# Attention's and memory's parts added by GpSimd instead of VectorE, with a newly searched instruction order

## The chip, the cores and the metric

The kernel runs on one core of a Trainium2 chip. The metric is the device time in microseconds (us) of one execution. Five engines work side by side, each through its own queue in order: TensorE (PE in the profile; PEld is its weight loads), VectorE (DVE), ScalarE (ACT), GpSimd (POOL) and SyncE (SP, which here only starts DMAs). SBUF is the on-chip memory, PSUM the memory that matmuls write. bf16 is a 16-bit float.

## The reference

Two independent parts share one output of 2048 x 1280. Part A (the first 640 columns) is a short convolution of `k`, a product with `v`, a convolution over the whole sequence done with FFTs, and a product with `q`. Part B (the last 640) is attention in four segments of 512 tokens, 32 heads of 20, with a memory that carries over from the earlier segments:

```python
for s in range(N):                       # N = 4 segments, L = 512
    logits = einsum('bhqd,bhkd->bhqk', qs, ks) * scale + mask
    p = softmax(logits)
    a_dot = einsum('bhqk,bhkd->bhqd', p, vs)
    pq = phi(qs)                         # phi(t) = t + 1 if t > 0 else exp(t)
    num = einsum('bhld,bhde->bhle', pq, M)
    den = einsum('bhld,bhd->bhl', pq, z) + 1e-06
    a_mem = num / den
    o = g * a_mem + (1.0 - g) * a_dot    # g = sigmoid(beta), one per head
    ...
    M = M + einsum('bhld,bhle->bhde', phi(ks), vs)
    z = z + sum(phi(ks))
return o @ wo
```

In segment 0 the memory is empty, so the sum `o` has one part only. In segments 1 to 3 it has two: these are the sums of the title.

## The kernel before, in words

A recording layer first collects all instructions, with what each depends on. Then two tables of numbers, `ORDER` and `BASE`, found by a search over a planner's costs, set the order in which they are issued on all engines and the PSUM banks they use. Every instruction is issued by one helper, so the profile shows line 256 for nearly all; tiles tell them apart. A third table, `EVICT`, says for each of the 227 copies from PSUM to SBUF whether DVE ("1") or ACT ("0") makes it.

Part A runs in five blocks of 128 columns (`conv`). `kr`, `kb` and `skd` are the short convolution, `vt` its product with v; `F` holds the spectrum as it leaves PSUM, `Xh` and `Kh` the two spectra after butterflies, `Y` and `pq` their product, and a last pass multiplies by q into `pq`, which a DMA writes out. All the butterflies and products are DVE work, mostly on two SBUF tensors of 1024 to 4096 elements in each partition.

Part B runs in eight units (`u`: segment `s`, half of the heads). `project` makes k and q (`KQ`) and v (`Va`) by matmul, copies them out of PSUM, and turns k and q around by DMA (`KQT`); `PP` and `PqT` are phi of k and q, `qabs`, `kam` and `A` a bound for the softmax. `attend` fills PSUM with logits, ACT takes their exponential into `ET` (128x1024 at a time, 160 of them), and PE multiplies by `Va` and by the memory `Mbd`. For each group of four heads `normalise` closes: a reciprocal of the denominators (`rr`), one product from PSUM into `o2` (the profile calls this tile `o`; it holds both parts, 2 x 320 elements, there is one buffer of it), and the sum of the two halves into `o_s`. `project_out` turns `o_s` around (by DMA in segments 0 to 2, by PE with the identity in the last, into `xT`), multiplies by `wo` and copies the result into `outb`, in the last segment also into `PP`, for the DMA out.

The sum stands once in each of the six units of segments 1 to 3 for each of the four groups of heads, so 24 times. POOL has only start-up work before the change: four DMAs (`outb` first receives beta, `qabs` the short filter) and the memsets.

Of the kernel before, what the change touches and what calls it, by code (L numbers as in the profile page):

```python
# [264 lines left out]
class Layer:  # L265
# [482 lines left out]
    def attend(self, u):  # L748
        nc, rec = self.nc, self.rec
        V = nc.vector  # L750
        s, half = u // 2, u % 2
# [114 lines left out]
        def normalise(gg, g, nb, step):  # L866
            rec.key = ("N", u, gg)
            h0 = 16 * half + 4 * gg
            pov = g.ap[:, 0:nb, 0:352].rearrange("p b (x e) -> p b x e", e=VW)
            rr = self.ring("rr", [128, 66], f32)[:, 0:16 * nb].rearrange("p (b x) -> p b x", x=16)  # L870
            den = pov[:, :, :, 0]
            part, bank, cell = [list(x) for x in den.ap] if nb > 1 else (None, None, None)
            if nb > 1:
                den = bass.AP(tensor=den.tensor, offset=den.offset, ap=[part, [512 + step, nb], cell])
            V.reciprocal(out=rr, in_=den, grp=g)
            num = pov[:, :, :, 1:DH + 1]
            if s == 0:
                dst = o_s[:, :, h0:h0 + 4 * nb, :].rearrange("p q (b h) e -> p b q h e", b=nb)
                V.tensor_tensor(out=dst, in0=num.rearrange("p b (q h) e -> p b q h e", h=4), in1=rr.rearrange("p b (q h) -> p b q h", h=4)[:, :, :, :, None].to_broadcast([128, nb, 4, 4, DH]), op=ALU.mult, grp=g)
            else:  # L880
                o2 = self.ring("o2", [128, 2, 16, DH])
# [28 lines left out]
    def project_out(self, s):  # L910
# [79 lines left out]
ORDER = r"""  # L990
c-jTQ17H{c3<SVW@|kUSwr$&9XWO=I+qOCz?QGk&&ATkf3P(0%M-JpfB;*2+A7v2{xlszyP#Mut0p(B)QBfLIkOyf{0A)}JF%S!R5gFwXfH=s2il~Yx2!(toh~!!cDO3<2hCE8dL`}p-UhRT(S{Oy32t
+Mp)lA5yDK&#uM-6mCDy@S=NR8S^fb5zU^^jg0pc(3-FEXPm3Tu57(dGz^Bxr>;D5~*L0vWYCiXn%#Kr*yOBNWpn$fs?QTYI7*ifcc#L<#MU#^`~P+7wwd9onH6@@s1CgZAivuo#H6nnpXKKZ>H14n=Z
wMkmBYLKM;hIvAz3j1IzR3`0&Gf{{ptFc^Tb7=z&$g|a$LGwBo^hY=W$;uxm0wV;;MZJ4f^bvr8PaNU9OI#yGnfo8;JghMW!fT=nWlduz$F-OPg6g1S5n2xzxRV!*Eor+32Pj_Lwj?fvXrqy+VPQyqIL
JfVam9>`cM->g!QCd@HVmA(;jyBfC+C)cdZQYAmSg6gluI|AiZL0gQM4Raht*7;M4rb~>oJ0#fgxOfC9rP5E;w&cX7@e<M(NSBf+5&B*=P(zMq?4L0)6)pSJoME0I0M=d{L<dqS{Gos_ENXwXrn81A!c
be{jJfghc3cOU5fCw1t+iq6Lpn#*Q02w%P>i!$T4iv)w&!}EV{MVc6t~~5Y-~sAKk2Lw2uzZff`wY(OK7Oc=Xl3dL3PLF}i42izYX5AN_QY4%YMNua|HE>-8cw>Sb)u+X!b@Fhn2XD&kpeTc=TFHEv+2
-oj%%!Wuk599xMnwnv}h0m4aiiEOJ7L*m+c+`(RbhW#2-_UT>3w}W~Q8<4=(B9<kx1G-J0ql2wOfQjwUv)a*KAdbY6xUv!3^(D^fCM32XJ+E6ep2U_U_6l3HpLMdG+TS``YYQ*CHNLz-1RT*_n$%t+x&
2dEB1tUC?2xvxcQ~r2G%=3pTLj2yO<`yBum)=q3DM))My}}zeUFrOQa_-lwX_IwU2o`Rjc73}m0iOpw6fH4MI+fqT-D@qK|dp=rI3{J6)hw^5?Vy*ZeP&LE^2DKq@gU0+|;}J4QcF_-qZUU+HPwqNo$#
{xAm|e$ZARDjy}+T_>PB~#gfS{q?JCFK+;JzODK;tyZyya46t;T#|GMOw3Qr2NpE?ri)FBGme2mcCA|!>u9nd<*-#s1Z7qYev;5XkAbDkwWs(9`&_o7XU&|+jETiO>!lrV`ikL}G3nh7ExMh|Rmdmn8Q
E4YRrLYu~+?HQPS}_YPqbvoATQMmjB`lYWu?|wwidrEVYc;Kal(Ovd-2$z>WtGx4)5cjXt7h$Gmc6tbGTuJe536Cq>h{ViTXC6SVdSGJe_9u*VkKmv^^mGoN+#K4`(<UVla!RM(oK5G6dP@wrJPl;^7h
)EXm=?sQ>~1Il{fa!Dp?<yX8ok1^%Zcom6N&FU&`1gt8I1cv(>dZHr-}eDAu#r+EVJ<GY!oKw$K{cb8T#8rJ=piCf3vzSu=Z~i_O`PVc6W}SvZE}5Sec+?5%#Ym-^lo*gO4eN2NWNTX?o$BYv^+(t#1V  # L1000
!iGvq4v>|$#8z20S#1?$jXl+Y^3@`-lB~7gw#=5Aah<i2KUPs9GXl38d0Yb7jK^fXRhIhPU^{Jx?X~8tDh(Kgy(B94+ddm6(K$jkS~b~Zn{A|=kRXf3+T3DQq_=FfT{c{*%O3lxHRP=gk{EoiyX~DFww
SCf!PZ(rtS!H5U1`T7_Ct@_E3GBRY_J@+nml0Nv=$FqO^L;LJY;d$ij8@~x^s%mkU*&;+iaAaw9|IR&RQFuv(YkE;_`!bVQY?&_-w+d(vjn2lGI^rcI9}PCm(gDbmC-5!1LCWb$QAb$b9L>3)VyuahjZ
!gq$v?Bq@7vp`4eK(o~Z3qW#p)?8)9dCv&8pB;zcZE3>5!FGv6zNn$491Ubz5l7fpQCHt}-8%RGkmc!Ce`tvPQ@f}lhAk*;$(=a`k%1aJlT4vx9SuBH?k$L!@gLzRhF)#CRnLJ}=HkajcNt#I^e&BsRX
JJ0%1LkKDKH>@~z#GiUUR)_dn2p()gSS|amn~R|G7EF^CWrI1tdiR-&RiVEGctn3Sb{_Og{4`BWjT_$xmwEczFd{^tiV#dD{JH_OY)OGkZV$rW4Tt!_(b{2&w5YpSS40w6;|aqe&%?N;t_enb@GkXc*X
8oS-)kkIEJJ7gZFq@Ub8xH%LbXi8m#5F?TTENpPa;*EbQy$i%w*q&tehZD6<(Nb2ynd<c@5Yn=+MiS=4`V9&gDsPT?k*!H@jSivEe4Wjc3AG5^Eswu+VfhCP(kEahvsO&-Zs`Od$b&jnn_MO@6%{*PN^
E#X13j_X;&mvAY?E4%x0uHa5t$;WbsHT|uqKamZ5CQs!qzsoMUXH|S7H*vSTlV=vzpUYKyA@pV3BhT%nY~>HRX5rm@ue_4_{#wHMHtv(ntmkheh}*e?A7u+0_)fl;lKw$<v626j&+<t^`B(WR`=zmekp
uFWVf>r?mI%I^q5YvX@ja~TH|+`kNJM{Rk$f-raX%w_RDWVo`~VN~sa5x;p3?uxAvW{WUcvuLIgjS4yoKMlU`F?t{=#B;Y>(rj&=~%}%6l?T?#=y>#Pt;3(yMwrZ{-IijVJJgp2$txc!0<Ew4T^cQ}wZ
>^J<>n&+sIVFo|dMOrF6{F@#5%#oKvS&*s@Zhf~k8hiCSr-r9S)>oMl^T;A4u`enBF;|#5N`~<Hsly>yIp3fV4ZqM%>yptFAa}1*eyt8-l^9-k5J*-|}3Ge0wy|#zfI^Nr(X?MTKe%{~v_$3bTfj-Im`
c+2IK|a|F`CuR8Q+&0L^N2dshxu?H;n%pv$9q&A;$uCEuJkxM!K3R)ALXljhDX-KI?-qQb;i|MKF8<!XrJeiG>K02`99MZ_*!4*F*K%5^JE%NW9f8X=!-moF7_q9)R*~kkFD!{g>UdZ9$%B{5l^UleWP
#oM7qfXG|2b)Q9tGfeT(n+t$xUl`(Z!e+kJ<h@L=EOJ3YjA`ELIYeKp$N  # L1010
"""
# [76 lines left out]
```

## Time and profile before

| | |
|---|---|
| time, median of 3 runs | 271.66 us (271.04 to 272.06) |
| profiled execution, span | 271.3 us; no other time is given for it |
| PE, DVE, ACT, POOL busy | 96%, 91%, 92%, 3% |
| granted TensorE clock | 1.000 |
| DVE: `o` products | 24, 820 ns mean |
| DVE: `o_s` sums of `o` | 24, 316 ns mean |
| ACT: `ET` exponentials | 160, 1113 ns mean |

The profile's busy time is the time in which an engine has at least one instruction under way. Instructions of one engine overlap a little: the next starts before the one ahead has ended. What an instruction costs its engine in a full stretch is therefore read from start to start, and is less than its duration. A row of the timeline gives the start (us), the time (us; several merged ones together), the engine, the line, the operation, out<-in, shapes and a count.

### The profile page before, as it was taken

What the parts mean: (1) busy time and instruction counts of PE and PEld (TensorE: products, weight loads), DVE (VectorE), ACT (ScalarE), POOL (GpSimd) and SP (SyncE); (2) the same over time, 40 slices, a digit from 0 to 9 for tenths busy, and PEclk for the clock granted to TensorE, in tenths of its full rate; (3) what the DMA queues carried; (4) which work ended last, traced back from release to release, by engine and by line L of the source; (5) the groups of instructions that cost most, each with busy time, mean ns of one, the idle gap of its engine ahead of it and who ended that gap; (6) DMA issues with size and microseconds to landing.
All of it is one profiled execution on the core that took longest, in us unless ns stands there. A gap on an engine that the chain in (4) does not pass through costs nothing.

```text
span 271.3 us, 10053 instructions
## 1 busy us (share of the span) xinstructions
PE 259.8 (96%) x4335; PEld 194.0 (71%) x4335; DVE 246.4 (91%) x385; ACT 249.7 (92%) x394; POOL 7.2 (3%) x18
## 2 busy tenths in 40 slices
PE   6999999999999999999999999999999999988994
PEld 2688768877767677877767788778776776565772
DVE  0268999999999999999999999999999999999972
ACT  2676899999899999999999999999999999999952
POOL 8200000000000000000000000000000000000000
PEclk9999999999999999999999999999999999999999
DMA  6997989999999869997997679996970094635124
GB/s 196 274 217 143 235 178 208 190 243 258 211 164 262 189 153 169 156 183 153 172 219 156 180 148 216 162 170 123 201 165 17 30 159 99 154 89 126 47 51 126
DMA packets 131516, 44.72 MB, mean 165 GB/s; under 512 B 121899, under 2 KB 129072, under 8 KB 131344
## 3 DMA queue, kind: packets, MB, share of 16 engines
q1 hardware_dynamic: 131328, 43.96, 80.0%
q8 instruction: 34, 0.56, 0.9%
q0 software_dynamic: 144, 0.12, 0.2%
q14 instruction: 10, 0.08, 0.1%
HBM read 14.05 MB, written 7.34 MB: 79 GB/s over the span
## 4 chain that ended last, share of the span: by engine, by line
PE 66%; ACT 18%; DMA 8%; SPq 3%; issue 2%; DVE 2%; ACTq 0%; DVEq 0%
PE ps L256 66%; ACT ET L256 12%; DMA Wi<-c_wi 3%; SPq L256 3%; ACT F L256 2%; DMA Y<-in_B_x_dram 2%; DMA KQT<-qabs 1%; ACT Va L256 1%; DMA pq<-in_A_q_dram 1%; ACT outb L256 1%; ACT KQ L256 1%; DVE PP L256 1%; ACT PP L256 1%; DVE o L256 0%; DVE outb L256 0%
## 5 line engine op out<-in xcount | busy, mean ns | idle before, releaser
L256 ACT ACTIVATE ET<-ps 128x1024 bf16<-128x1024 f32 x160 | 162.4, 1113 | 0.4 <-PE ps L256 0.4
L256 PE MATMUL ps<-wqkv,xT 128*128 128x320 bf16 x480 | 78.2, 302 | 0.6 <-ACT ET L256 0.3
L256 PEld LDWEIGHTS <-xT 128*128 128x128 bf16 x640 | 58.0, 98 | 28.8 <-issue 7.1
L256 ACT CAST F<-ps 128x512 bf16<-128x512 f32 x72 | 43.9, 683 | 1.3 <-PE ps L256 1.3
L256 PE MATMUL ps<-Va,ET 128*128 128x21 bf16 x1280 | 41.9, 173 | 0.0
L256 PEld LDWEIGHTS <-ET 128*128 128x128 bf16 x1280 | 39.3, 96 | 3.3 <-issue 2.1
L256 PE MATMUL ps<-KQT 32*128 32x128 bf16 (+2 forms) x896 | 34.8, 239 | 0.6 <-DMA KQT<-qabs 0.4
L256 PEld LDWEIGHTS <-Wf 128*128 128x128 bf16 x320 | 29.6, 98 | 6.5 <-issue 1.6
L256 ACT CAST KQ<-ps 128x320 bf16<-128x320 f32 x56 | 26.7, 522 | 1.8 <-PE ps L256 1.8
L256 PE MATMUL ps<-wo,xT 128*128 128x320 bf16 (+2 forms) x160 | 25.5, 299 | 1.3 <-ACT ET L256 1.3
L256 PEld LDWEIGHTS <-KQT 32*128 32x128 bf16 x896 | 16.5, 92 | 10.1 <-issue 7.6
L256 PE MATMUL ps<-kT,Wf 128*128 128x256 bf16 x160 | 22.2, 273 | 0.0
L256 PE MATMUL ps<-vt,Wf 128*128 128x256 bf16 x160 | 21.6, 273 | 0.2
L256 PE MATMUL ps<-Y,Wi 128*128 128x256 bf16 x160 | 20.8, 273 | 0.8 <-DMA Wi<-c_wi 0.8
L256 DVE TENSOR_TENSOR o<-ps,rr 128x640 bf16<-128x640 f32 x24 | 19.7, 820 | 0.4
L256 PE MATMUL ps<-Mbd,PqT 128*128 128x84 bf16 x96 | 18.3, 202 | 1.1 <-ACT ET L256 1.0
L256 DVE TENSOR_TENSOR Y<-Y,pq 128x2048 bf16<-128x2048 bf16 (+1 forms) x20 | 18.6, 943 | 0.0
L256 DVE TENSOR_TENSOR pq<-Xh,Kh 128x2048 bf16<-128x2048 bf16 x15 | 18.3, 1219 | 0.0
L256 ACT CAST Va<-ps 128x320 bf16<-128x320 f32 x31 | 16.0, 536 | 2.2 <-PE ps L256 2.2
L256 PEld LDWEIGHTS <-Wi 128*128 128x128 bf16 x160 | 14.7, 98 | 3.5 <-DMA Wi<-c_wi 1.0
L256 PE MATMUL ps<-skd,kr 128*128 128x128 bf16 (+4 forms) x116 | 16.7, 257 | 0.0
L256 PEld LDWEIGHTS <-kr 128*128 128x128 bf16 x116 | 14.8, 149 | 2.3 <-issue 1.0
(86 smaller groups left out, 363.2 us busy)
## 6 DMA issues: line engine op xcount, KB each, us to landing
vt<-in_A_v_dram SPq DMA_DIRECT2D x10, 256.0 KB
pq<-in_A_q_dram SPq DMA_DIRECT2D x10, 256.0 KB
turned<-kT SPq DMA_DIRECT2D x4, 512.0 KB
kT<-turned SPq DMA_DIRECT2D x8, 256.0 KB
out_dram<-pq SPq DMA_DIRECT2D x8, 256.0 KB
out_dram<-outb SPq DMA_DIRECT2D x12, 160.0 KB
kb<-kr SPq DMA_DIRECT2D x6, 256.0 KB
Wf<-c_wf SPq DMA_DIRECT2D x4, 256.0 KB
```

The source lines that it names most:

```text
L256: f(*[fix(a) for a in args], **{k: fix(v) for k, v in kw.items()})
```

## The change

One instruction moves from DVE to POOL, with 600 ns as its price in the planner. Then the order, the banks and the copies' engines were searched anew, so that instructions stand elsewhere on every engine.

```diff
@@ normalise (segments 1 to 3)
                 V.tensor_tensor(out=o2[:], in0=num, in1=rr[:, :, :, None].to_broadcast([128, 2, 16, DH]), op=ALU.mult, grp=g)
-                V.tensor_tensor(out=o_s[:, :, h0:h0 + 4, :], in0=o2[:, 0].rearrange("p (q h) e -> p q h e", h=4), in1=o2[:, 1].rearrange("p (q h) e -> p q h e", h=4), op=ALU.add)
+                nc.gpsimd.tensor_tensor(out=o_s[:, :, h0:h0 + 4, :], dur=600, in0=o2[:, 0].rearrange("p (q h) e -> p q h e", h=4), in1=o2[:, 1].rearrange("p (q h) e -> p q h e", h=4), op=ALU.add)
@@ tables
-EVICT = ("11000000110000001000000010000000...
+EVICT = ("11010101000010000100010000000000...
-ORDER = c-jTQ17H{c3<SVW@|kUSwr$&9XWO=I+qOCz?QGk&&ATkf3P(0...
+ORDER = c-jrq17i>h7zNOKKjd1rYuUDKFWa_l+sk$>+qP}n=6mNqoXp6...
-BASE = c-mc30g?nD2qH86|Bo*b+ufU{GBZNd04x~%&bTx0ns;wsVABs...
+BASE = c-l>q2@*pg2txru?|<X!Bii2?>Vi!|pv%I{hSd(=5qmfHF0~sw...
```

Counted over the whole program, DVE loses the 24 sums and takes over copies from ACT: `KQ` 8 becomes 12, `Va` 1 becomes 5, `xT` of 512 elements 1 becomes 4, `xT` of 640 1 becomes 2, `kT` 1 becomes 2. In the other direction `outb` of 320 elements goes from 8 on DVE to 4, and the one of 512 from DVE to ACT. PE and SP have the same instructions as before in another order.

DVE in segment 1, before: the `o` product, then the sum two rows behind it.

```order
L256 TENSOR_SCALAR qabs_74<-KQ 128x1280
L256 TENSOR_TENSOR o_79<-ps,rr_101 128x640
L256 TENSOR_TENSOR pq_111<-Xh_110,Kh_108 128x2048
L256 TENSOR_TENSOR o_s_115<-o_79 128x4x80
L256 CAST outb_75<-ps 128x320
L256 RECIPROCAL rr_101<-ps 128x32
L256 TENSOR_TENSOR PP<-PP,qabs_74 128x64x20
L256 TENSOR_TENSOR o_79<-ps,rr_101 128x640
```

DVE in segment 1, now: the fifth of the 24 places (`ps` is PSUM; the other tiles lie in SBUF).

```order
L256 RECIPROCAL rr_101<-ps 128x32
L256 TENSOR_TENSOR o_79<-ps,rr_101 128x640
L256 TENSOR_TENSOR pq_111<-Xh_110,Kh_108 128x2048
L256 CAST Va_90<-ps 128x16x20
L256 TENSOR_SCALAR qabs_74<-KQ 128x1280
L256 TENSOR_TENSOR qabs_74<-qabs_74 128x640
L256 TENSOR_TENSOR Xh_110<-Xh_110,Kh_108 128x2048
```

The sum has gone from DVE's queue, and what stood behind it follows at once. In 17 of the 24 places the row behind the `o` product reads SBUF alone; in the other 7 it reads PSUM.

POOL at the start of the program, as a piece of the difference.

```order
+L256 DMA pack<-c_pack 128x448
+L256 DMA qabs_74<-in_A_shift_k_dram 5x512
+L256 MEMSET PP 128x128x12
 L256 DMA outb_75<-in_B_beta_dram 1x16x2
-L256 DMA qabs_74<-in_A_shift_k_dram 5x512
-L256 DMA pack<-c_pack 128x448
 L256 MEMSET KQ 128x128x12
```

Beta's DMA has moved from the first place to the fourth, behind two DMAs and a memset. At the end of POOL's queue one `ISA` row and the 24 sums follow the memsets, and nothing else. On PE, the ten warm-up matmuls on `o` now all stand ahead of the filter's and beta's matmuls, the beta matmul (`outb`) stands between the filter's and the transposes of x (`Y`), and ten `wqkv` matmuls fewer stand ahead of the first logits.

DVE at the end of the program, before.

```order
L256 RECIPROCAL rr_101<-ps 128x32
L256 TENSOR_TENSOR o_79<-ps,rr_101 128x640
L256 TENSOR_TENSOR o_s_115<-o_79 128x4x80
L256 TENSOR_TENSOR pq_111<-ps,pq_111 128x4x128
L256 CAST outb_76<-ps 128x512
L256 CAST PP<-ps 128x512
```

And now.

```order
L256 RECIPROCAL rr_101<-ps 128x32
L256 TENSOR_TENSOR o_79<-ps,rr_101 128x640
L256 TENSOR_TENSOR pq_111<-ps,pq_111 128x4x128
L256 CAST xT_103<-ps 128x512
L256 CAST PP<-ps 128x512
```

The last sum is POOL's, and the copy of the last turned `o_s` (`xT`) DVE's. On PE, 9 matmuls of `wo` with 512 columns are left at the very end where 11 were.

More of the change, by code (lines that the diff above doesn't have):

```diff
@@ L986 @@
 TAP2 = (2, 3, 4)
-EVICT = ("11000000110000001000000010000000000000000000000000000000000000100000000000001000010001001010100100100000000000000000110000000000000010000000"
-         "000000000101000100100100000000000000000000001100001000000000000000000000010110010000011")
+EVICT = ("11010101000010000100010000000000000000000000000000000000000000001000001000000000001011000100000100000000000000000000000000010000000000000000"
+         "000000000000100110111000000000010000010000110000000001100011011000000001101001111000010")
@@ L989 @@
 KQW, FW, WW = 1, 1, 1
 ORDER = r"""
[L991 to L1010, printed above, removed]
+c-jrq17i>h7zNOKKjd1rYuUDKFWa_l+sk$>+qP}n=6mNqoXp6AtjLD!$bl$`h@8lU+;F4?5D9sZ7g13O`A`}8Q65!L0ntzfWl<3YkQ%uq9%7;-sv?WjKq-_%9MncCBt%W5l~5>+TF8j#sD|WXNCZI))PW)Z1rZrR
@@ new lines @@
+h=uBCj7(^VbP_08r77}AAtCCcIU1ld>LNYrp(P4S5h;Ww=!!0AhF)lmZb&ahB{W(f3|gU>G(r#bMjK?46jEF=NL-YV;>a$2kXPEG15%<Vx}&7@MSHYEehEZMDT=}vgaODWr6dW`pc67n3FMN&7=mHwh$2WMW6%!;
+Whh2r1o|U~48#~2j<6^#TQC-*QAS20rxcLMG7hOESdyWv#K%;bBB^DLl$Qk9hKY!c`chHK$uyaOSu$1{$WWOr<FOT!Fd4(7p-e$I>_!!-Dtl2~reP1JqMB5Y8nO>TGESyrJ9Z$WjF*~{NoHUtD#<Q{ptjVK=~72#
+Vu3uCVwfS7<uvNaER2+c7$t`=TqZ~(Stxa7HqKzKG?NiBPZ~>enJDe$EHa>lERtX(#U$B?Cel$lNK<Jk^W_{)VzHdUT+G2tSt328m$Z`6auhvfskD}55?SYAxok!xc9r=!j$`;EQ8cV>!V2jo-Q@(r>0ddFBiJCz
+upbA|MiyYDEJ9lek5#f-*2qG%lc*X^f5|#ojPSYyA#xsT<u2As1nneC@mnq+9lA(oxrCb#y@>vzYC1q%Zy~l0l-_a=eI%Cll`z^*BJ&Cc$u0@tWek=$dL37>5;1kR?2)y&ja7)J4>3gU<0<0ma>UnlNT_#k1CQ|l
@@ new lines @@
+&#(e}C6PYD6GUYcuEujj;~MOfS9pp2l32IMRteC)O6{i`@B*>9P2%vZoRjkslO6R9l4w$Guj{c<VllaP(zp!Ac<i8?BsyC&nQoWY2+z&3Lt5!S*(nF4wH^`ZQ3=!(8iVg}N>0mL9F*idBxfY09+osr%VTm}0(niY
+;kvZY_lT&8c|%fbOFbcN7)kr<W%+<49H3XEhbHAo`G_=nRk~?U4W$V*881k8y(yn?R|acn?WLdb6{$1=qw5!3l8bUr{vkfU;g-bE@5rQyabFVfwmgs@_>Ih(kg50+Su`RO@s6Zs3ij4M`cP6bx8~Kf+FAb~k3N#D
++C{T#I{k$<+ExeZApHwrdL63im`%Y9YRsrZG$Yef*_NS5=FohaU!7gG07EmU=F)bWi<dM53ur+ts>O7;4%0l$#!M`vPb4o#XmQQV!kV2$w1gJnNX^IG%)x>z%0m37`B_qPa<rDx_N<{}bgcf=b}UR-kdD)0r2Wze
+7_VVCQEO^d?Z62-LyNN{XR6pF?aXRgT|a3h?ZU}gf*tu;t7s>N<x71lWwf$pWhuVWck)`Zu&ln8(ww5@wVamLH(Hhzv@5&wyH?b0oTX(rO5ey2ovI)7qXz42t);bfnoid`+Jm93t{&wJsi&c=q1M;Fd@1j>kv7(T
@@ new lines @@
+EXTjvK!<Y#=WAGNqR06~n`#(as0*|=2eO%d)#et?=4g4kJ(b_uhc&IazL!C4VRLn<R%8Xv(-rzhzv)V?Wvg_xF4tu`l;LeKhp{<_aE&g~wHm?RY9+qY#s3$JXf3!^o7xgJ`!4ltyEd~(R)s$#z_w{m_F@Cutqm=*
+J(H@eZ<V=M*Xst|qfx9HLv*8V(*8Wg=MvRwbDa+04&AI@WtT>?>TF{>HLiV=nv8C3?UfwV7<O2L*vM*FJUgO?v=)P`owejq-KXvCm~PS7R);m%!CLXS?$-kv$6DG*j^YWe%P}0yQ#`FHa8l1`H#@8Kcur60365iD
+i)FQ~mBqBF>}WH2UdQr+*0JeqY}44ql4CsQaTe!r2D{oxPUd{hWqeC$-K{a3@Pj0<+59L6Z6c@eEPL2R4Q5iC#JYBxy)3!4wsTBo=h?}6TOvEd`fOqsnAmRE1op8&Yrwvi#8TJ`Tfnz=(^6VLOJy%DjWy&VrnYyM
+))uqBHDWp&VCgM`<+hBL$1>SKduW3!uNAbOwvhMjy*;wa+LVQ?8Hd>e%V)Q2DKpy;D{KYqndP@EmerQ<gWa~FHrTS+b6d_Lmfdn#F&l10?W=u~gUo5gZG<i3Px)fG?6X|tC4RF~R@zF~7+b-TR>sEJQ!8tSSkCTp
@@ new lines @@
+tX<|EePiWqr2VkF`q@_UmfqtPmh{n9+JD+@9c5*_l;7ugt7s2c$yTwlO|&Yun!jufuX2J_u&P$guJJbS@VEW3b^IdNImvGDuT8O=ysFpq7AyHZTgwVw*{j=nPPVCbU1wNDpJ~%<8~@oX3*mH|Z8sDiY%7eul|_65
+S6Lx1>MKorj;TN7JbT3XwuPH{gbQr7752Hd&>q`Pny<BuJj_M5*w)xm+r%gK%64(N?dCFjZR_kYzgu-*Z%eF(@8Mf+u(1Aw@3@`eJ;+0B2i?Q@M{c%Fw#7EuR@-JZ{WYKRraog`-^)+Dr=fhi)$<*;%U*CFciS88
+u`BwVVSKOcv(WyP_5B;)^E*Fqr~P0A|H+8H-(InVe`Z5}qSgEhe=)$HX(WHDRs1)jcw~RB2P}oB@;g@E_p_@1Wh4K`vfkLEdP=`*(Y=XB^N&`}UowWr^jKcU53s3!vSc3UFZ2&%dmNAJ4>h^pS4eY@@2Ne3KhlKW
+%pYhXZ{de5t)I3uPHE{4Jh8{~be_ap`58;^C+(DF@vPq3Gk8YN=Gk2(lXv&Wn$!<lX7Ax5IXtJEwDVl<(!tw%Pd{SEte79Qj-K1|_*pCNc|Ek`^W)apPgp4F<YA<Zck%q*%?o&24=d-atM~F+UeLoyc<JM{y|4H4
@@ L1011 @@
+^VZw@`v9Nl1AVezwLw0~qsnNHC=ukcU9d4e#G}Yqk0z1jiVgK)KHNw6H5=^X{GyHYmA=Zydu*BDkz~5Zk;F37XZa;dBBOk^$CKzX!>4$FtoC4!A=ho1ukkq^U*`I9U*J=Hq0jTUvdHKAVqf7)e7~>trM}D)NG#dv
+M|{1n^O%xUHh73{^hC1BkNPoBDBFCqCzCCH+z<G6Kj=Grm!I(6e#m$FVc+9>eV_ja$miPL
 """
 BASE = r"""
-c-mc30g?nD2qH86|Bo*b+ufU{GBZNd04x~%&bTx0ns;wsVABs;$<=x9*NVF?t;Ty0?OflYUD3Gb!~1n-SztuovFZ0a%3nVn{+bWf7}IF|!Wq-Cbp|81egJP%FUlJ9#&+Ewa@gcwoXgX1piGB#NSVe1Z7
-0j|`_r$^hloyAF7=j}SF{nubYqGhY`pU!(^71UT~`EBq%wiD=vp+R*`dGMHyr10V|G)~t!(p)1DFq#c|1h>mj{$>l4UaQMP1|7!ijx2k_=};DARxb^!(-D85-4S<oHp`pO&L-aEJU;E2C;o9?dM(N%2P
@@ L1015 @@
-eL%ljRj%R<czI6%p)#R4aCDcowH>04x9xzou9#VIJQ7uy^I{pB12L?C
+c-l>q2@*pg2txru?|<X!Bii2?>Vi!|pv%I{hSd(=5qmfHF0~swn|m!=dtL8t?tHRa+^&6dR@43BeeKghb8b)W{K8=~ID&IyPgZ9&ahy~CathbUB@BV)1f{tHEiR2+Pw--Zu|PHP^=H74C~3sj@AAOJFjQTiOo$Wb
+3Z4O~^Ia$~s=w7;--4Y>v#ILNO=)QjgEs^G1fj?_cHr?O^3$0qzd~4{e0Su;?M|}V>v~sddR6S}_0`mo?&*|Q69<bbjA*A9hy{lWy(cI>ivGAJO?M)%&pj8dbAi;F9FED0RG8R@+z2@}UUq7R{LSMc{vBKLp`@*(
+vKg-CP{%q<|CpW*r?<%jjZby<Iu#Ew<)^8GDPN0l9J@~a09>mE9{
 """
```

## The prediction

> **What bounds the kernel now.** I read the shares of busy time first, then the same by stage, cut where ACT starts its first `ET` (36.2 us) and ends its last (260.6), then the waits inside the middle stage, then the timeline.
>
> ```profile
> PE 259.8 (96%) x4335; PEld 194.0 (71%) x4335; DVE 246.4 (91%) x385; ACT 249.7 (92%) x394; POOL 7.2 (3%) x18
> ...
> 0.00:36.20 36.20, 33.70 (x279) 24.03 (x280) 21.30 (x38) 23.52 (x58) 7.21 (x18) 1.00 0.89 209
> 36.20:260.60 224.40, 218.92 (x3970) 165.57 (x3971) 221.21 (x342) 223.23 (x332) 0.00 (x0) 1.00 0.82 161
> 260.60:271.30 10.70, 7.21 (x90) 4.39 (x87) 3.92 (x8) 2.92 (x5) 0.00 (x0) 1.00 0.37 100
> ...
> DVE rr L256 <- PE ps L256: 0.5, 1, 0.5
> ...
> ACT F L256 <- PE ps L256: 0.7, 1, 0.7
> ...
> PE ps L256 <- ACT ET L256: 3.4, 10, 0.5
> ```
>
> The window columns are length, then PE, PEld, DVE, ACT and POOL. In the middle 224.4 us ACT is idle for 1.2 us and DVE for 3.2 us (224.4 less 223.23 and 221.21). No wait of either is longer than 0.7 us. PE's largest wait there is for ACT's `ET`. That PE too reads 218.9 says less, since its ends are modelled and its instructions overlap. So two engines are full at once, and the timeline shows that they are truly back to back:
>
> ```profile
> 44.61 1.22 DVE L256 TENSOR_TENSOR pq<-Xh,Kh 128x2048 bf16<-128x2048 bf16 x1
> 45.74 1.29 DVE L256 TENSOR_TENSOR vt<-ps,vt 128x512 bf16<-128x512 f32 x2
> ...
> 48.88 0.50 DVE L256 TENSOR_SCALAR qabs<-KQ 128x1280 int16<-128x1280 int16 x1
> 49.28 1.23 DVE L256 TENSOR_TENSOR pq<-Xh,Kh 128x2048 bf16<-128x2048 bf16 x1
> ...
> 43.87 0.50 ACT L256 CAST Va<-ps 128x320 bf16<-128x320 f32 x1
> 44.17 1.12 ACT L256 ACTIVATE ET<-ps 128x1024 bf16<-128x1024 f32 x1
> 45.09 1.36 ACT L256 ACTIVATE PP<-KQ 128x1280 bf16<-128x1280 bf16 x1
> ...
> 48.36 1.22 ACT L256 CAST F<-ps 128x512 bf16<-128x512 f32 x2
> 49.31 0.49 ACT L256 ACTIVATE skd<-pack,taps 128x64 bf16<-128x64 bf16 x1
> 49.56 1.16 ACT L256 ACTIVATE ET<-ps 128x1024 bf16<-128x1024 f32 x1
> ```
>
> From start to start the 1.22 us product costs DVE 1.13, the 0.50 us scalar row 0.40; on ACT an `ET` costs 0.92, a `Va` copy 0.30, a 512-wide copy 0.48, an `skd` 0.25. The time moves only if the middle stage gets shorter for DVE and ACT both, or longer for one of them.
>
> **The change part by part.** All sums are against the profiled execution, span 271.3 us; the median of the runs, 271.66, lies 0.36 above it, which I add at the end.
>
> *DVE in the middle stage, the direct part.* Start-to-start costs from the end of the stage:
>
> ```profile
> 252.12 0.48 DVE L256 CAST outb<-ps 128x320 bf16<-128x320 f32 x1
> 252.52 0.68 DVE L256 TENSOR_TENSOR Y<-Xh 128x1024 bf16<-128x1024 bf16 x1
> 253.12 0.32 DVE L256 TENSOR_TENSOR o_s<-o 128x320 bf16<-128x320 bf16 x1
> 253.36 0.69 DVE L256 TENSOR_TENSOR Y<-Xh 128x1024 bf16<-128x1024 bf16 x1
> ...
> 259.52 0.68 DVE L256 CAST xT<-ps 128x512 bf16<-128x512 f32 x1
> 260.12 0.68 DVE L256 TENSOR_TENSOR pq<-ps,pq 128x512 bf16<-128x512 f32 x1
> ```
>
> A sum costs 0.24 us, a 320-wide copy 0.40, a 512-wide one 0.60. 22 of the 24 sums lie in the stage (the last two start after 260.6): -5.3. In the changed order DVE has there 6 `KQ` and 4 `Va` copies more and 4 `outb` fewer, 6 x 0.40, and one `xT` more, 0.60: +3.0. Net -2.3.
>
> *ACT in the middle stage.* 5 `KQ` and 3 `Va` fewer, 4 `outb` more (all 320 wide): -4 x 0.30; 2 `xT` fewer: -1.0; one `skd` and one small copy more: +0.4. Net -1.8. So if nothing else happened, both full engines would lose about 2 us.
>
> *POOL's sums and what they do to DVE.* Before, POOL does no arithmetic, and its last row, a memset, starts at 8.13 us, so two things are unknown: how long a sum takes there, and whether DVE runs on beside it. The nearest rows:
>
> ```profile
> 5.29 0.40 POOL L256 MEMSET Mbd<- 128x336 bf16 x1
> 5.61 0.54 POOL L256 MEMSET qabs<- 128x512 bf16 x1
> ...
> 7.99 0.13 POOL L256 MEMSET kb<- 128x16 bf16 x1
> 8.00 0.82 DVE L256 CAST xT<-ps 128x640 bf16<-128x640 f32 x1 [1.72 <-PE ps L256]
> 8.13 0.38 POOL L256 MEMSET PP<- 128x64 bf16 x1
> ```
>
> A memset of 336 elements holds POOL for 0.32 us from start to start and only writes; a sum of 320 reads two inputs and writes one. Bounds: 0.3 us (the pace of one pass) and 0.9 (three passes). I take 0.6, two passes, since the two reads and not the write are what differs from the memset. On the second question the rows say one thing: a DVE copy out of PSUM ran with two POOL memsets inside it and took 0.82 us, no more than the `o` product of the same 640 elements out of PSUM (0.82 in the row at 262.27 below). For DVE rows that read SBUF alone nothing is shown. The bounds there are no hold at all, and a hold of a DVE row until the sum is done.
>
> I take the hold. POOL's part starts when the `o` product is complete, while the DVE row behind it is already under way; the sum then runs behind that row if it reads SBUF alone, and the next such row waits. I went through the 24 places in the changed order with the start-to-start costs above and 0.6 us for a sum. In 11 places two SBUF rows follow one another and the second waits the whole 0.6; in 8 a copy, a reciprocal or a PSUM product covers part (at the fifth place, shown with the change, `pq`, then a `Va` copy of 0.40, then `qabs` waits 0.2); in 5 nothing waits. In sum 8.3 us; with 0.3 us for a sum 3.4, with 0.9 us 14.3.
>
> [...]
>
> *Sum for the stage.* DVE -2.3 + 8.3 = +6.0. Its 3.2 us of idle time can take part of that; I give it all of them: +2.8. ACT's 1.8 is then worth nothing, because DVE ends last. The wait that grows is ACT's and PE's for DVE: PSUM banks that DVE must empty (`vt`, `o`, `F`) come free later, and the `ET` queue behind them dries up.
>
> *Waits that the change adds.* There is one `o` buffer, so the next `o` product waits for POOL's sum. The closest two that matter stand four DVE rows apart, with `PP` (1280 elements, between the 0.60 of 1024 and the 1.13 of 2048), a reciprocal and a scalar row (0.40) between: over 1.1 us against 0.6 plus a hand-over, covered. It would cost a few tenths at that one place if the sum starts only behind `PP`. The readers of `o_s` in segments 0 to 2 are DMAs planned well behind. POOL's queue holds nothing else by then.
>
> *Start.*
>
> ```profile
> 1.25 0.64 POOL L256 DMA_DIRECT2D outb<-in_B_beta_dram  x1 [0.81 <-POOLq L1072]
> 1.88 0.52 POOL L256 DMA_DIRECT2D qabs<-in_A_shift_k_dram  x1
> 2.40 0.58 POOL L256 DMA_DIRECT2D pack<-c_pack  x1
> ...
> 6.67 1.40 POOL L256 MEMSET PP<- 128x1536 bf16 x1
> ...
> 4.59 0.18 PE L256 MATMUL ps<-outb,ident 1*128 1x32 bf16 x1 [0.60 <-DMA outb<-in_B_beta_dram]
> ...
> 6.18 0.71 PE L256 MATMUL ps<-ident,Y 128*128 128x128 bf16 x5
> 7.25 1.04 PE L256 MATMUL ps<-ident,Y 128*128 128x128 bf16 x8 [0.36 <-DMA Y<-in_B_x_dram]
> ...
> 31.39 4.23 PE L256 MATMUL ps<-wqkv,xT 128*128 128x320 bf16 x30
> ```
>
> Beta's DMA now starts behind 0.58, 0.52 and 1.32 (the memset less its overlap), at 3.7 instead of 1.25, and lands 3.3 later as before: 7.0. The beta matmul stands ahead of the `Y` transposes, the first of which ran at 6.18, so the second group starts at about 7.9 instead of 7.25: up to +0.6. Against it, ten `wqkv` matmuls fewer stand ahead of the first logits (the 30 at 31.39 took 4.23 us, so -1.4 at most). I count 0 and keep +0.6 and -1.4.
>
> *End.*
>
> ```profile
> 262.27 0.82 DVE L256 TENSOR_TENSOR o<-ps,rr 128x640 bf16<-128x640 f32 x1
> 263.13 0.32 DVE L256 TENSOR_TENSOR o_s<-o 128x320 bf16<-128x320 bf16 x1
> ...
> 263.51 0.40 PE L256 MATMUL ps<-ident,o_s 128*128 128x128 bf16 x4
> 263.75 4.06 PE L256 MATMUL ps<-wo,xT 128*128 128x512 bf16 x24
> ```
>
> Here the last sum is on the path: 0.38 us from its start to PE's. On POOL that is 0.6 plus the same hand-over, +0.3 to +0.4. Two 512-wide `wo` matmuls fewer follow: 24 of mixed width, worth 18 full ones, in 4.06 is 0.22 each, -0.4. Nil.
>
> Sum: 271.3 + 2.8 = 274.1, and with the 0.36 above it 274.5.
>
> **The rivals.**
>
> *Side by side (faster).* DVE does not notice POOL's reads. Then the stage shrinks by the smaller relief, ACT's 1.8, to 269.9, and to 268.5 if the start gives its 1.4. The copy at 8.00 speaks for it, weakly; that 17 of 24 sums meet rows which read both inputs from SBUF, of which the trace has no example, leaves it open. It decides if a sum holds DVE for less than about 0.2 us: (2.3 + 3.2) / 24.
>
> *A draw.* A sum is as short as the memset, 0.3 us, and holds 3.4 us in all: DVE +1.1, inside its 3.2 of idle time, and ACT's relief is eaten by the same places. 270.3 to 273.0.
>
> *Long sums (slower still).* At 0.9 us DVE gains 14.3 - 2.3 - 3.2 = 8.8 of work: 280.4.
>
> *The order decides, not the sums.* The order is new everywhere. With 1.2 and 3.2 us idle before, it can hardly pack the middle stage tighter; it can pack it looser. That is inside the ranges of the others.
>
> **How the numbers follow.** About 0.5%, 1.4 us, is what a measurement can tell from no change here. Forecast (hold of some 0.5 to 0.7 us; 273.0 to 277.5): 0.41. Long sums: 0.09. Draw: 0.17. Side by side, with the order as good as before: 0.33. So slower 0.50, same 0.17, faster 0.33. The forecast's own range is 273.0 to 277.5. The range for 8 in 10 leaves out the long sums and the part of the faster case below 269.0 (about 0.1): 269.0 to 277.5.
>
> **What would show it.** Right: in the changed profile POOL has 24 rows of about 0.6 us, and some 19 DVE rows with SBUF inputs close to them are longer than elsewhere, or start late; DVE stays full in the middle while ACT's idle time there rises by several us, waiting on PE. Wrong: the products `pq<-Xh,Kh` keep 1.13 us from start to start with a POOL sum inside them, ACT's idle time stays near 1 us, and its last `ET` ends about 2 us earlier. A start that has moved by more than 1 us, or a last sum that takes over 0.8 us to reach PE, would show those terms mis-sized.

## The result, and the profile after

The changed kernel takes 282.83 us (median of 4 runs, 280.42 to 284.68), the kernel before 271.35 beside it: a ratio of 1.0387, 95% interval 1.0330 to 1.0445. The forecast was 274.5, with a range of 269.0 to 277.5. Medians below are of all runs shown; the ratios leave disturbed runs out. The profiled execution after has a span of 282.3 us and a time of 284.1.

First the page of the kernel after (busy time, the granted clock in 40 slices, two groups), then its three stages, cut as before at ACT's first and last `ET`:

```profile
PE 264.0 (94%) x4333; PEld 195.7 (69%) x4335; DVE 253.9 (90%) x369; ACT 249.5 (88%) x386; POOL 36.1 (13%) x42
...
PEclk9799999999959999999999999999999999979999
...
L256 POOL TENSOR_TENSOR o_s<-o 128x320 bf16<-128x320 bf16 x24 | 29.0, 1207 | 237.5 <-DVE o L256 237.5
```

```profile
0.00:35.19 35.19, 31.49 (x271) 22.92 (x272) 21.84 (x38) 22.04 (x55) 7.14 (x18) 0.95 0.82 204
35.19:271.27 236.08, 225.16 (x3973) 168.21 (x3972) 227.93 (x326) 224.62 (x328) 27.38 (x22) 0.98 0.79 155
271.27:282.30 11.03, 7.37 (x95) 4.58 (x93) 4.10 (x7) 2.83 (x5) 1.58 (x2) 0.99 0.35 95
```

The start is 1.0 us shorter, the end 0.3 longer, the middle 11.7 longer (224.4 before): that is the span's +11.0. In the middle DVE has 6.7 us more of work (227.93 against 221.21), and its idle time has not shrunk but grown, from 3.2 to 8.15 (236.08 less 227.93). ACT, with 1.4 more of work, is idle for 11.5 instead of 1.2. The waits of that stage (in total, times, longest):

```profile
ACT ET L256 <- PE ps L256: 7.5, 12, 2.8
...
DVE kam L256 <- ACT KQ L256: 2.5, 1, 2.5
PE ps L256 <- DMA kr<-kr: 2.4, 1, 2.4
PE ps L256 <- ACT ET L256: 2.2, 5, 0.5
DVE vt L256 <- PE ps L256: 2.0, 2, 1.5
PE ps L256 <- DVE o L256: 1.8, 4, 0.9
```

ACT's queue of `ET` now runs dry behind PE, as the forecast said. But no engine is the bound throughout: each waits for another in turn. The forecast's sign "DVE stays full in the middle" did not come.

The hold can be read off the timeline. Four places in the kernel after:

```profile
140.30 0.97 POOL L256 TENSOR_TENSOR o_s<-o 128x320 bf16<-128x320 bf16 x1 [1.71 <-DVE o L256]
140.54 1.81 DVE L256 TENSOR_TENSOR pq<-Xh,Kh 128x2048 bf16<-128x2048 bf16 x1
142.28 0.48 DVE L256 CAST KQ<-ps 128x320 bf16<-128x320 f32 x1
...
224.68 1.17 POOL L256 TENSOR_TENSOR o_s<-o 128x320 bf16<-128x320 bf16 x1 [8.55 <-DVE o L256]
225.12 0.68 DVE L256 TENSOR_TENSOR pq<-ps,pq 128x512 bf16<-128x512 f32 x1
...
228.15 1.17 POOL L256 TENSOR_TENSOR o_s<-o 128x320 bf16<-128x320 bf16 x1 [2.30 <-DVE o L256]
228.59 1.08 DVE L256 TENSOR_SCALAR qabs<-KQ 128x1280 int16<-128x1280 int16 x1
...
242.50 2.28 DVE L256 TENSOR_TENSOR Y<-Xh,Kh 128x4096 bf16<-128x4096 bf16 x1
242.66 2.77 POOL L256 TENSOR_TENSOR o_s<-o 128x320 bf16<-128x320 bf16 x1 [2.63 <-DVE o L256]
244.70 1.81 DVE L256 TENSOR_TENSOR pq<-Xh,Kh 128x2048 bf16<-128x2048 bf16 x1
```

The product `pq<-Xh,Kh` takes 1.81 us instead of 1.22, the scalar row 1.08 instead of 0.48: 0.60 more each. The row at 225.12, which reads one input from PSUM, takes its usual 0.68 beside a sum. And at 242.66 the sum itself waits for the long row that was first (2.28 us, not lengthened), lasts 2.77 us with that wait, and then holds the next one for 0.6. A sum that meets nothing takes 0.79 us; the mean of the 24, waits included, is 1.21. Over the 24 sums, 19 DVE rows grew (by over 0.1 us each against the same row elsewhere), 9 of them by the whole 0.6, and all of them by 8.33 us.

### The profile page after: what moved, and what is told of

The parts are those of the page before. It is cut to its first block, busy times and chain, and to the rows that moved or that the text cites. A ratio compares the mean times of both kernels' runs of the same rounds, so it can differ in the third digit from the quotient of the medians.

```text
span 282.3 us, 10081 instructions
## 1 busy us (share of the span) xinstructions
PE 264.0 (94%) x4333; PEld 195.7 (69%) x4335; DVE 253.9 (90%) x369; ACT 249.5 (88%) x386; POOL 36.1 (13%) x42
## 4 chain that ended last, share of the span: by engine, by line
DVE 22%; PE 18%; issue 7%; ACT 2%; DMA 1%; POOLq 0%; POOL 0%; DVEq 0%; ACTq 0%
PE ps L256 18%; DVE Xh L256 4%; DVE o L256 3%; DVE Y L256 3%; DVE pq L256 3%; DVE qabs L256 2%; ACT ET L256 1%; DVE F L256 1%; DVE rr L256 1%; DVE Kh L256 1%; DMA pq<-in_A_q_dram 1%; DVE vt L256 1%; ACT F L256 1%; DVE KQ L256 1%; DVE PP L256 1%
## 5 line engine op out<-in xcount | busy, mean ns | idle before, releaser
L256 ACT ACTIVATE ET<-ps 128x1024 bf16<-128x1024 f32 x160 | 158.1, 1058 | 8.0 <-PE ps L256 7.5
L256 PE MATMUL ps<-wqkv,xT 128*128 128x320 bf16 x480 | 79.3, 306 | 1.0 <-DVE o L256 0.3
L256 PEld LDWEIGHTS <-xT 128*128 128x128 bf16 x640 | 59.6, 100 | 29.7 <-issue 6.6
L256 POOL TENSOR_TENSOR o_s<-o 128x320 bf16<-128x320 bf16 x24 | 29.0, 1207 | 237.5 <-DVE o L256 237.5
L256 PE MATMUL ps<-Va,ET 128*128 128x21 bf16 x1280 | 42.5, 173 | 0.0
L256 ACT CAST F<-ps 128x512 bf16<-128x512 f32 x72 | 40.4, 640 | 1.2 <-DVE F L256 1.2
L256 PE MATMUL ps<-wo,xT 128*128 128x320 bf16 (+2 forms) x159 | 26.8, 309 | 1.4 <-ACT ET L256 1.0
L256 ACT CAST KQ<-ps 128x320 bf16<-128x320 f32 x52 | 22.8, 468 | 4.2 <-PE ps L256 3.8
L256 PE MATMUL ps<-kT,Wf 128*128 128x256 bf16 x160 | 20.8, 273 | 0.1
L256 DVE TENSOR_TENSOR pq<-Xh,Kh 128x2048 bf16<-128x2048 bf16 x15 | 20.5, 1365 | 0.1
```

Source lines behind the costliest of these rows:

```text
L256: f(*[fix(a) for a in args], **{k: fix(v) for k, v in kw.items()})
```

## The experiments

All are compared with the kernel before, run beside them: 272.41 us for the first four, 271.72 for the next four, 271.88 and 272.33 for the last two pairs.

### The order without the sums, and the sums without the order

e1: the changed kernel with the sums back on VectorE.

```diff
-                nc.gpsimd.tensor_tensor(out=o_s[:, :, h0:h0 + 4, :], dur=600, ...
+                V.tensor_tensor(out=o_s[:, :, h0:h0 + 4, :], ...
```

> The changed kernel with its order, banks and copies as they are, the 24 sums alone back on VectorE. Theory 1 (two causes: the sums' hold on VectorE costs 5 to 6 us, the new order's late kr transfer at 75 to 84 us and the halved clock behind it 5 us): 276 to 277. Theory 2 (the sums alone; the stall at 75 us is made good later): 270 to 272. Theory 3 (the order alone; the holds lie in idle time): 281 to 283.

e2: the kernel before with the opposite edit, all 24 sums on GpSimd in the old order.

> The kernel before with its own order, the 24 sums alone moved to GpSimd. VectorE loses 24 x 0.24 = 5.7 us and gains holds of some 8 us. Theory 1: 273 to 277. Theory 2 (all 11 us are the sums'): 280 or more. Theory 3: 269 to 272.

e1 took 277.93 us (275.86 to 278.69), ratio 1.0205 (1.0147 to 1.0262); e2 273.89 (273.25 to 275.73), ratio 1.0079 (1.0050 to 1.0108). So about half of the loss is there without any sum on GpSimd: the new order and copies cost 5.5 us by themselves. That is the figure of one chip: e12, further down, is the same kernel on another, and 8.0 us above the kernel before beside it. e2 came out inside the range of its theory 1, e1 0.9 us above it. The sums cost 4.9 on the new order (282.83 less 277.93) and 1.5 on the old, where by the same count they hold DVE for 5.1 us, at other places.

The middle stages of e1 and, from below, of e5:

```profile
35.37:263.15 227.78, 221.84 (x3973) 166.67 (x3971) 224.54 (x348) 223.80 (x328) 0.00 (x0) 0.99 0.84 160
```

```profile
34.83:261.68 226.85, 221.16 (x3973) 166.36 (x3971) 220.73 (x326) 223.26 (x328) 15.99 (x44) 0.99 0.85 161
```

In e1's profiled execution (275.86, the shortest of its four) DVE has 3.3 us more of work than before and the old idle time, 3.2: the work went into the time one for one. The profile of e12 repeats it, with a stage of 227.81 us, 224.35 of it DVE's work. In e5 DVE and ACT have the work of the kernel before within 0.5 us (220.73 and 223.26 against 221.21 and 223.23), yet the stage is 2.5 us longer, with 6.1 and 3.6 us idle. So the added work fits as a part of the order's cost, and is not the whole.

### A transfer that PE waits for

In the kernel after, PE waits 2.4 us at 75.6 for the transfer `kr<-kr`, and the clock is then halved for 6.8 us. These rows are the stretch 72.00 to 84.13, after and before:

```profile
72.00:84.13 12.13, 9.64 (x151) 6.60 (x153) 8.19 (x13) 7.66 (x11) 0.00 (x0) 0.72 1.05 187
```

```profile
72.00:84.13 12.13, 11.80 (x202) 8.60 (x201) 12.07 (x21) 12.13 (x17) 0.00 (x0) 1.00 0.99 188
```

ACT and DVE lose some 4 us each there. SP had issued the transfer at 72.4 (before: 65.2), behind two others that waited for ACT. e3 moves it ahead of them; e4 does so with the sums on VectorE.

```diff
+    lc = [o.idx for o in rec.ops if o.key == ("A", 2, "lc")]       # kb, kb, kr
+    rows = [o.idx for o in rec.ops if o.key == ("rows", 1)]        # KQT<-qabs
...
+    order[at:at] = lc[0:2]          # ahead of the rows
...
+    order[at:at] = lc[2:3]          # right behind them
```

> The changed kernel, sums on GpSimd, with the two kb transfers of the third block moved ahead of the four KQT rows and the kr transfer right behind them on the DMA queue, so that PE should not wait for kr at 75 us and its clock should not fall there. Theory 1: 277 to 279. Theory 2: 281 to 283, no difference. Theory 3: 271 to 275.

> Both edits at once: sums on VectorE and the kr transfer early, in the changed order. Theory 1: 270 to 272.5, both causes gone. Theory 2: the same as with the sums alone back on VectorE. Theory 3: the same as with the early transfer alone.

e3 took 284.05 (281.65 to 285.22), ratio 1.0430 (1.0363 to 1.0498); e4 279.25 (277.37 to 280.17), ratio 1.0256 (1.0200 to 1.0313). Not faster than what they were made from: that theory fell. The wait for `kr` is gone from e3's profile, and so is the halved clock there (1.00 from 72 to 84 us), but PE waits for DVE instead (0.8 for `pq`, 0.5 for `o_s`). Nor is a wait of that length the order's own: in the same order, e1's profile shows none, e12's 0.2 us and e5's 1.2. The difference of the two is again 4.8 us for the sums. Within e3 the time follows the mean clock: 281.65 us at 0.994, 283.82 and 284.27 at 0.982, 285.22 at 0.970. Within e1 it does not: the longest run, 278.69, has the highest clock, 0.993.

### GpSimd that only writes

e5 keeps GpSimd's place in the order, and takes away its reads. It leaves the sum out, on both engines.

```diff
-                nc.gpsimd.tensor_tensor(out=o_s[:, :, h0:h0 + 4, :], dur=600, ...
+                with rec.one():
+                    nc.gpsimd.memset(o2[:, 0], 0.5)
+                    nc.gpsimd.memset(o_s[:, :, h0:h0 + 4, :], 0.5)
```

> The changed kernel, but in place of each of the 24 sums GpSimd makes two memsets, one over the first half of `o` (so that it still waits for the product and still keeps the one `o` buffer) and one over the slice of `o_s` that the sum would write. The sum is left out; GpSimd only writes. Theory (the hold is between GpSimd's reads of SBUF and VectorE's): the 8.66 us by which VectorE's rows grew are gone, `pq<-Xh,Kh` stays at 1.22 us beside a memset, and the time falls to 274 to 278. Rival 1 (any GpSimd access to SBUF holds VectorE for as long): rows grow by up to 0.6 us as before, 282 to 284. Rival 2 (the cost is the hand-over to GpSimd and the one `o` buffer, not the hold): rows keep their length and the time still stays at 281 to 284.

```profile
141.38 1.22 DVE L256 TENSOR_TENSOR pq<-Xh,Kh 128x2048 bf16<-128x2048 bf16 x1
141.52 0.36 POOL L256 MEMSET o<- 128x320 bf16 x1 [4.66 <-DVE o L256]
141.83 0.36 POOL L256 MEMSET o_s<- 128x320 bf16 x1
```

It is the place of 140.30 above: the product keeps its 1.22 us with two memsets inside it. Over the program no product grows, only two scalar rows, by 0.07 each. 275.87 us (272.94 to 278.75), where the changed kernel has 282.83: the reads, not the hand-over to GpSimd nor the one `o` buffer, are the sums' cost. And even its fastest run, with the sums gone from both engines, is above the median of the kernel before.

### Eight sums that hold nothing, eight that hold

Both on the old order; they differ only in which eight sums move.

```diff
+                E = nc.gpsimd if 4 * (u - 2) + gg in (1, 2, 7, 8, 9, 14, 21, 22) else V      # e7: (3, 4, 5, 6, 10, 15, 17, 18)
-                V.tensor_tensor(out=o_s[:, :, h0:h0 + 4, :], ...
+                E.tensor_tensor(out=o_s[:, :, h0:h0 + 4, :], ...
```

> The kernel before, its order and copies unchanged; 8 of the 24 sums on GpSimd, numbers 1, 2, 7, 8, 9, 14, 21 and 22 (from 0): those beside which no VectorE row grew when all 24 were moved in this order. Theory (the price of a moved sum is the hold in the next row): VectorE is freed of 8 x 0.24 = 1.9 us and held for under 0.3; ACT is as full as before, so the time comes out between 271.2 and 272.6, no slower than before (272.4). Rival (each moved sum costs the same, 1.5 us / 24, whatever stands beside it): +0.5, 272.9.

> As the run with eight sums moved, but numbers 3, 4, 5, 6, 10, 15, 17 and 18: those beside which rows grew most (3.7 us in all when 24 were moved). Theory: freed 1.9, held 3.7, net +1.8: 273.4 to 274.4. Rival (same cost for each moved sum): 272.9, no different from the other eight.

One place of e6, then one of e7 (two `Xh<-Y` rows merged: the second starts 1.13 us behind the first and takes 1.81):

```profile
130.92 1.22 DVE L256 TENSOR_TENSOR pq<-Xh,Kh 128x2048 bf16<-128x2048 bf16 x1
131.08 1.70 POOL L256 TENSOR_TENSOR o_s<-o 128x320 bf16<-128x320 bf16 x1 [13.51 <-DVE o L256]
132.05 0.48 DVE L256 CAST outb<-ps 128x320 bf16<-128x320 f32 x1
```

```profile
153.41 2.94 DVE L256 TENSOR_TENSOR Xh<-Y 128x2048 bf16<-128x2048 bf16 x2
153.57 1.70 POOL L256 TENSOR_TENSOR o_s<-o 128x320 bf16<-128x320 bf16 x1 [5.84 <-DVE o L256]
```

The same sum of 1.70 us on GpSimd costs DVE nothing where a copy out of PSUM follows, and 0.6 where a product does. e6: 271.93 us (270.72 to 275.20), ratio 1.0022 (0.9985 to 1.0060), no row grown. e7: 273.50 (272.84 to 277.25), ratio 1.0079 (1.0055 to 1.0103), rows grown by 3.66 in sum. The rival of one price for every sum gives 272.9 for both: e6 alone does not rule it out (0.5 us lies inside its interval), e7 does. The price is in the row that follows the sum. Also: in e6 1.9 us of DVE's work is freed at no cost, and the time does not fall.

### The order with other copies

e8 is e1 with the table `EVICT` of the kernel before, so that every engine has the old work in the new order; e9 is the mirror, the kernel before with the new table.

```diff
-EVICT = ("11010101000010000100010000000000...
+EVICT = ("11000000110000001000000010000000...
```

> The changed kernel's order and banks, but the table of copies of the kernel before, and the sums on VectorE: both engines have the work of the kernel before in the new order. Theory (the order's own +5.5 us are mostly the 3.0 us of copies that were given to VectorE for the sums taken from it): 274.3 to 275.5. Rival 1 (the order itself packs looser, the copies' engines do not matter): 277 to 279. Rival 2 (this order needs its own copies, others fall where the engine is late): above 279.

> The mirror of the run of the new order with the old copies: the order and banks of the kernel before, all sums on VectorE, and the table of copies of the changed kernel. VectorE has 3.0 us more of copies, ACT 1.2 to 1.8 us fewer. Theory (an order stands only with the copies it was searched with; a copy on the other engine is late where it falls, and the whole pipeline waits): well above the 3 us, 285 to 300. Rival (only the sum of the work counts): 272 + 3 = 275, or less where VectorE's 3.2 us of idle time take it up.

e8 took 302.00 us (298.04 to 303.93), ratio 1.1037 (1.0949 to 1.1125); e9 289.62 (287.39 to 290.07), ratio 1.0637 (1.0604 to 1.0671). My theory for e8, that the copies given to VectorE are most of the order's cost, fell by 27 us; its second rival, that the order needs its own copies, held, and so did the theory for e9. The stage of e8 and two of its waits:

```profile
40.50:291.35 250.85, 227.92 (x3973) 168.21 (x3971) 224.46 (x342) 227.71 (x335) 0.00 (x0) 0.97 0.76 145
```

```profile
ACT ET L256 <- PE ps L256: 10.9, 11, 3.5
DVE rr L256 <- PE ps L256: 9.3, 10, 2.1
```

DVE and ACT have 3.3 and 4.5 us more of busy time than before, in a stage 26 us longer; the rest is waiting, in many places. So in both directions the order did worse with the copies of the other one.

### A version meant to beat both

e10 is e6 with three copies beside the moved sums given from ACT to VectorE.

```diff
-        if EVICT[e] == "1":
+        if EVICT[e] == "1" or e in (120, 192, 196):
```

> A version meant to be faster than both: the kernel before with the eight sums on GpSimd that hold nothing, and three copies next to them (numbers 120, 192 and 196: one `outb`, one `KQ`, one `Va`) given from ACT to VectorE, so that both full engines lose work: VectorE -1.9 + 1.2 = -0.7 us, ACT -0.95. Theory: 270.8 to 271.6. Rival 1 (work taken from a full engine only turns into idle time, as with the eight sums alone): 271.5 to 272.5. Rival 2 (copies out of their order make it late): above 273.

273.75 us (271.04 to 275.44), ratio 1.0054 (1.0020 to 1.0089): not faster, although both full engines had less to do (in the stage of its profile DVE is busy for 220.82 us and ACT for 222.69, with 4.6 and 2.7 idle). The theory was missed, and the time is that of the second rival, copies out of their order. No version found here beats the kernel before.

### PE's thin stretch

In six profiles of the new order with its own copies (the kernel after, e1, e3, e4, e5 and e12) the clock is halved for some 3.4 us late in the program: its mean is 0.79 from 238 to 246 us in e1, e5 and e12, 0.89 from 246 to 262 in the kernel after, and 0.94 from 235 to 265 in e3 and e4. In e1 it comes at 242.0, behind three small groups of logits for which PE waited 0.4, 0.5 and 0.3 us. e11 fills those gaps: one logits group is computed five times.

```diff
+            more = [c for c in o.calls if c[4].idx == 444] * 4 if i == 1398 else []
-            for eng, method, args, kw, grp in o.calls:
+            for eng, method, args, kw, grp in o.calls + more:
```

> The changed order and copies with the sums on VectorE (277.9), and 16 logits matmuls more: at 239 to 241 us, where PE waits 0.4 and 0.5 us between two small groups and the clock is then halved for 3.4 us, one `KQT` group whose exponential comes last is computed five times instead of once (the same values, 0.8 us of PE's waiting time). Theory (PE's thin stretch brings the half clock, and that is a part of the order's own cost): the profile shows the full clock at 241 to 246, the `wqkv` matmuls there take 0.76 instead of 1.54 us for five, and the median falls by 1 to 1.5, to 276.4 to 277. Rival 1 (the half clock comes whatever PE does there): unchanged, 277.9 to 278.2. Rival 2 (it goes, but is worth nothing, as another engine is the bound there): full clock, same time.

e12 is e1 again, as its measure.

> The changed order and copies with the sums on VectorE once more, on the same chip as the run with the filled gaps, as its measure: 277 to 279, with a half clock at 241 to 246 in its profile.

PE at that place and the window 238 to 246, first of e11, then of e12:

```profile
239.43 1.27 PE L257 MATMUL ps<-KQT 32*128 32x384 bf16 x26 [0.37 <-ACT ET L257]
...
242.67 0.84 PE L257 MATMUL ps<-wqkv,xT 128*128 128x320 bf16 x5
```

```profile
238.00:246.00 8.00, 7.01 (x171) 5.25 (x162) 7.93 (x12) 7.81 (x11) 0.00 (x0) 1.00 0.66 93
```

```profile
239.53 0.34 PE L256 MATMUL ps<-KQT 32*128 32x384 bf16 x2 [0.52 <-ACT ET L256]
...
243.06 1.30 PE L256 MATMUL ps<-wqkv,xT 128*128 128x320 bf16 x5
```

```profile
238.00:246.00 8.00, 6.83 (x116) 4.34 (x113) 7.39 (x10) 6.85 (x10) 0.00 (x0) 0.79 0.55 64
```

With more to do, PE keeps its full clock, and ACT is busy for 7.81 of the 8 us instead of 6.85. The ten `ET` rows from number 140 to 150 take 10.8 us there, against 11.9 in e12 and 11.7 in e1 (10.4 before). So at this place PE's thin work brings the halved clock, as far as one profile of e11 can show, and the ten rows lose 1.0 us by it. But little of this reaches the end: the stages of the two profiles are 227.20 and 227.81 us long, and the executions took 275.15 and 275.25. The medians are 279.38 (275.15 to 280.80) and 280.34 (275.25 to 281.64), the ratios 1.0105 (1.0052 to 1.0157) and 1.0262 (1.0208 to 1.0317); the two shortest executions of each, 275.15 and 275.62 against 275.25 and 277.11, overlap. So the local gain is shown, and a gain in the whole time is not. Both medians lie above what was expected, 276.4 to 277 and 277 to 279.

## Why the prediction was wrong

The direction was right, and the hold that was forecast is there. But the sums are only about half of the loss; the other half comes with the new order and copies, which the prediction named and did not price. The forecast was 8.3 us too low, and the time is outside the range. Point by point:

- **The hold.** That a sum which reads SBUF holds DVE was a choice between two bounds, which no row of the profile before showed; the kernel after and e7 show it, and e5, with no reads, has no product grown. Right in kind: the rows behind the sums are held, and by how much depends on the row. Taken 0.6 us a place and 8.3 in all, 11 places whole and 8 in part; measured 0.60 and 8.33, 9 whole and 10 in part. That the two agree so well is partly luck: 0.6 was taken as the sum's duration, all of which holds. The sum takes 0.79, of which 0.19 holds nothing; by the prediction's own count, 0.79 would have made the hold some 12 us.
- **DVE's work.** Forecast +6.0 in the middle, measured +6.7.
- **"Its 3.2 us of idle time can take part of that; I give it all of them": the first step that failed.** DVE's idle time is 8.15 us after. With some 3 us of work added it was still 3.2 in e1, 2.9 in e11 and 3.5 in e12, and where sums were moved it lay above that, from 4.1 (e2) to 8.15. It can be larger with no sum moved, too: 7.1 in e4. Nowhere here did added work use it up. That work added at one place comes out behind it, while the idle time lies elsewhere and stays, is my reading of this. With the old idle time kept, the middle would have been forecast 6.0 longer; it is 11.7 longer, 6.7 of work and 5.0 of new waits.
- **"That is inside the ranges of the others": the second.** The rival that the order decides was named, and dismissed without a price. e1 gives it: +5.5 us, about half of the loss (e12: +8.0). By the prediction's own terms this kernel has 3.0 us of copies more on DVE and 3.2 of idle time to take them, so nothing. The two failed steps overlap here: those 3.0 are part of the 5.5. I argued that an order with so little idle time can pack looser only a little, and put it into a range that the sums had made.
- **ACT's relief of 1.8.** It did not come. In e5, without holds, ACT is busy for 223.26 us in the stage, 223.23 before. Added up from start to start, its other rows in the stage cost 1.0 less, but the 159 `ET` behind the first cost 146.8 instead of 145.8. A row with a gap behind it counts in full, without the overlap (in the kernel before, an `ET` of 1.12 us cost 0.92 from start to start); that there are more such `ET` rows (8 instead of 2) fits this, but does not settle it. So the rival "side by side" was priced wrong too: e5 comes closest to that case, and took 272.94 to 278.75 where 269.9 was forecast.
- **Start and end.** Counted 0 with +0.6 and -1.4 kept: -1.0. The end, nil: from the last `o` product 9.0 us before, 9.1 after. The last sum:

```profile
273.20 0.82 DVE L256 TENSOR_TENSOR o<-ps,rr 128x640 bf16<-128x640 f32 x1
...
274.10 0.79 POOL L256 TENSOR_TENSOR o_s<-o 128x320 bf16<-128x320 bf16 x1 [1.53 <-DVE o L256]
...
274.95 0.40 PE L256 MATMUL ps<-ident,o_s 128*128 128x128 bf16 x4
```

  0.85 us from its start to PE's, 0.38 before: +0.47, where 0.3 to 0.4 was forecast. That is 0.05 past the 0.8 us which the prediction named as the sign of a mis-sized term.
- **The 0.36 from the span to the median.** In every later execution the time lies 1.7 to 1.9 us above its own span (284.1 and 282.3, for one). The execution with a span of 271.3 thus took about 273.1, some 1.4 more than the median, and 0.36 is not the distance from a span to its time. The forecast is not changed by it, since 271.3 and 0.36 are the median itself, to which the 2.8 were added.

How the 11.5 us divide, by the medians: 5.5 for order and copies (e1); 4.9 for the sums on this order; the other 1.1 is the difference between the two medians of the kernel before (271.35 and 272.41). Of the 4.9, 2.9 are the hold less the freed work (8.33 less the 5.4 that 22 sums cost DVE in e1, start to start), and the remaining 2.0 are put down to the waits that it sets off. e2 shows the like: hold and freed work are about equal there (5.1 each), and it is 1.5 longer.

What the order's part is made of is open beyond this. The added work of DVE fits as a part: the profiles of e1 and e12 have 3.3 and 3.1 us more, and stages longer by 3.4 each. It is not all: e5, with the old amounts of work, is 4.2 above the kernel before by the medians. It is not the transfer `kr` (e1, e3), and filling one thin stretch of PE moved the profiled execution by 0.1 (e11). The runs of the new order have a lower mean clock (0.968 to 0.993 in e1 and e12, against 0.992 to 1.000 beside them), and in e12 the two shortest runs, 275.25 and 277.11, have the highest, 0.988 and 0.987. Further halved stretches would fit; whether they cause the longer runs or come with them is not shown. Filling every thin stretch of PE was not tried.

## What to carry to other kernels

Before giving GpSimd a read of SBUF, look at the row that stands behind it on VectorE: here it cost up to 0.6 of its 0.79 us where a product of two SBUF inputs or a scalar row had to wait, and nothing where a row that reads PSUM followed (0.68 us at 225.12, as elsewhere). Price a newly searched order as a change of its own, by running it with the moved work put back; the prices in this kernel's source give each instruction a fixed duration and have no term for a hold or for a halved clock, and with engines this full the order lost as much as the sums. Measure it on more than one chip: 5.5 and 8.0 us here. And do not count idle time as room for more work unless it lies at the place where the work is added.

## What the runs showed of the hardware

- GpSimd's hold was the same at each of the nine whole places: 0.59 to 0.60 us of a 0.79 us sum, on products and on a one-input scalar row alike. Two memsets there held no product (e5: `pq<-Xh,Kh` 1.22 us), and two scalar rows by 0.07 us each.
- In the kernel after, the granted clock was 0.50 in three stretches: 3.4 us at 9.0 and at 247.9, and twice that, 6.8, at 77.3. It was halved not only behind one long wait: PE had waited 1.7 us at 77.3, but in e12 it ran three logits groups in the 2 us ahead, with waits of 0.3 to 0.5 us. With sixteen small matmuls more in those gaps it stayed full (e11, one profile: 1.00 from 238 to 246, against 0.79 in e12).
- With 56 of the 227 copies on the other engine than the order was searched with, e8 took 24 us more than e1 (302.00 and 277.93), and e9 18 more than the kernel before (289.62 and 271.88).
